# Attention and a feed-forward network in one kernel: the tiles that TensorE streams begin 64 bytes beyond its weights, modulo 256

## The chip, the cores and the metric

The kernel runs on one core of one Trainium2 chip. Its time is the device time of one launch in microseconds; three runs of the kernel before gave 839.77, 840.28 and 840.65 us, median 840.28 us.

## The reference

Four batch elements, 12 heads, 448 positions, head size 64; the model width is 768, and the feed-forward network is 3072 wide. All data are float32.

```
scores = q @ k^T / sqrt(64), causal mask, softmax over keys
x      = (softmax @ v), heads side by side          # (4, 448, 768)
xn     = (x - mean) / sqrt(var + 1e-6) * g_ln
out    = x + relu(xn @ w_ch1) @ w_ch2               # 768 -> 3072 -> 768
```

## The kernel before

**Products.** Every matrix is split into a high part and a low part of type float32r (`xh` and `xl`, `hh` and `hl`, `wh` and `wl`), and a product of two matrices is three matmuls into one PSUM bank: high by high, high weights by low data, low weights by high data. TensorE first loads a 128x128 weight tile (the stationary operand: LDWEIGHTS, PEld in the profile) and then streams the data past it (the moving operand, 448 or 450 columns of 4 bytes in each partition). Each matmul has a weight load of its own; the load of the next matmul runs while the present one streams.

**Stages.** Batches 0 and 1 run the plain network (function `ffn`): `ph` is the first product (data `xh`, `xl`), `po` the second (data `hh`, `hl`). In batch 0 `xh` and `xl` have 450 columns, two of them sums for the normalisation, and in batch 1 448. Batches 2 and 3 run together (class `Pair`) as seven products of sums and differences (Strassen's scheme); there the banks are `bX`, `bY`, `bA`, the weights `wk` and `wp`, and the data are `xh` and `xl` again (two of the seven), the tiles `xT1h`, `xT1l` to `xT4h`, `xT4l`, `xB22h` and `xB22l`, and for the second layer `h1` and `h2` (shown as `h`) and four tiles `hx`. The attention of a batch (`sc` scores, `pt` transposes, `px` the product with v) is spread among the network's matmuls of earlier batches.

**Order.** Nothing here is ordered by the hardware: the program is recorded whole (class `Plan`), list-scheduled by a table of costs on the five engines' queues, and written out in that order. All instructions carry the line of the recording helper (L553), so the profile is read by tiles. The change does not touch the costs or the dependences that the planner sees.

**Places in SBUF.** A tile pool gives each tile a fixed byte address in every partition, one after another. The two small tiles `least` and `ve`, and the big ones `xh` and `xl`, stand ahead of others in this row, so their sizes set the addresses of what follows. A product's chunk `c` begins 448 x 4 = 1792 bytes (7 x 256) after the one before it, so all chunks of a 448-column tile begin at the same byte modulo 256; with 450 columns each chunk begins 1800 bytes after the one before, 8 bytes further modulo 256. Weight chunks are 512 bytes long.

Of the kernel before, what the change touches and what calls it, by code (L numbers as in the profile page):

```python
# [11 lines left out]
F32 = mybir.dt.float32  # L12
F32R = mybir.dt.float32r
# [10 lines left out]
P = 128  # L24
C = 112
NC = S // C
NP = H // 2
KC = DM // P
# [533 lines left out]
def kernel(ctx, tc, qk, v, w1, w2, g, out):  # L562
# [3 lines left out]
    def pool(name, bufs, **kw):  # L566
        return Pool(plan, name, bufs, **kw)
# [6 lines left out]
    const = pool("const", 1)  # L574
    sb = pool("sb", 1)
# [18 lines left out]
    ident = identr.bitcast(F32)  # L594
    warm = const.tile([P, 1], BF16, name="warm")
    sums = const.tile([C, 5, 3, 4], F32, name="sums")
    least = const.tile([C, 6, 2], F32, name="least")
    mask = ap.tile([C, S], BF16, name="mask")
    g_sb = const.tile([P, KC + 1], F32, name="g_sb")
    g_sb, part = g_sb[:, :KC], g_sb[:, KC:]  # L600
# [79 lines left out]
    def move(dst, src):  # L680
        nc.either(
            ("scalar", "activation", (), dict(out=dst, in_=src, func=ACTF.Copy)),
            ("vector", "tensor_copy", (dst, src), {}),
        )
# [47 lines left out]
    class Att:  # L732
# [7 lines left out]

        def parts(self):
            n = S + 2 if self.b == 0 else S
            self.xh = sb.tile([P, KC, n], F32R, tag="xh", name="xh", bufs=1)
            self.xl = sb.tile([P, KC, n], F32R, tag="xl", name="xl", bufs=1)

        def columns(self):

# [257 lines left out]
        def squares(self):  # L1005
            if self.b in (1, 2):
                mb = self.spread_one(self.t["mv"])
                if self.b in MBS:
                    mb, wide = ap.tile([P, S], F32, tag="PT", name="mbs", bufs=8), mb
                    move(mb, wide)  # L1010
            else:
                mb = self.t["mb"] if self.b else self.mb
            some = [ap.tile([P, S], F32, tag="PT", name="xc", bufs=8) for _ in range(XC)]
            for c in range(KC):
                t = some[c % (XC - 1) + 1 if c else 0]
                nc.vector.tensor_tensor(out=t, in0=self.xT[c], in1=mb, op=ALU.subtract if self.b else ALU.add)
                nc.either(
                    ("scalar", "activation", (), dict(out=t, in_=t, func=ACTF.Square)),
                    ("gpsimd", "tensor_tensor", (), dict(out=t, in0=t, in1=t, op=ALU.mult)),
                )  # L1020
                if c:
                    self.add(acc, acc, t)
                else:
                    acc = t
            ve = sb.tile([C, NC], F32, tag="ve", name="ve", bufs=2)
            nc.vector.tensor_scalar_add(ve, self.small(acc, "var"), 1e-6)
            nc.gpsimd.tensor_tensor(out=ve, in0=ve, in1=mhalf, op=ALU.pow)
            self.t["ve"] = ve
# [575 lines left out]
```

## Time and profile before

| | kernel before |
|---|---|
| median of three runs | 840.28 us |
| span of the profiled execution, first to last instruction | 838.0 us |
| TensorE matmul busy | 830.5 us (99%), 4582 instructions |
| TensorE weight loads busy | 727.3 us |
| VectorE busy | 696.2 us (83%) |
| ScalarE busy | 513.0 us (61%) |
| GpSimd busy | 319.9 us (38%) |

The profiled execution's own time is its span; the launch around it is the 2.3 us by which the median stands above the span. TensorE's granted clock is at full in every slice of the page. A matmul's duration in the profile is its latency: the next one starts before it has ended, so what a matmul costs is the distance from its start to the start of the next one, and a run of matmuls is best read in the chain, where the pieces do not overlap.

### The profile page before, as it was taken

To read this page: it belongs to the slowest core of one execution; us is meant where nothing else is said; L and a number is where in the kernel's file an instruction comes from. 1 tells how busy PE (TensorE), PEld (TensorE's weight loads), DVE (VectorE), ACT (ScalarE), POOL (GpSimd) and SP (SyncE) were. 2 spreads that over 40 slices of the span, in tenths; PEclk is the share of its full clock that TensorE was granted. 3 is DMA by queue.
4 is the path that set the end of the run, shared out by engine and by line. 5 is a ranking of instruction groups with operands and counts; after the bars stand their busy time and mean duration, and the time that the engine had idled before them with its cause. 6 is when DMAs were issued, how large, how long until landed. Compare 5 with 4: busy or idle time off the path is not lost.

```text
span 838.0 us, 13712 instructions
## 1 busy us (share of the span) xinstructions
PE 830.5 (99%) x4582; PEld 727.3 (87%) x4582; DVE 696.2 (83%) x1445; ACT 513.0 (61%) x1129; POOL 319.9 (38%) x309
## 2 busy tenths in 40 slices
PE   9999999999999999999999999999999999999998
PEld 5679889888788898898989899999999898999997
DVE  6899999899999987877777489787887878778685
ACT  7999998888789675565454235543625435254450
POOL 5753111101452622421110378436446354554440
PEclk9999999999999999999999999999999999999999
DMA  9687888886778798769775464334243342423324
GB/s 200 257 298 257 316 281 313 319 298 252 268 268 299 236 332 274 275 221 293 241 232 191 149 200 136 117 101 123 74 138 95 103 121 85 147 74 116 117 92 149
DMA packets 61319, 168.79 MB, mean 201 GB/s; under 512 B 7009, under 2 KB 25825, under 8 KB 61249
## 3 DMA queue, kind: packets, MB, share of 16 engines
q1 hardware_dynamic: 61248, 167.92, 60.4%
q8 instruction: 36, 0.59, 0.3%
q14 instruction: 35, 0.28, 0.1%
HBM read 119.15 MB, written 39.71 MB: 190 GB/s over the span
## 4 chain that ended last, share of the span: by engine, by line
PE 95%; DVE 3%; ACT 1%; issue 0%; POOL 0%; ACTq 0%; POOLq 0%; DVEq 0%
PE po L553 21%; PE bX L553 21%; PE ph L553 21%; PE bY L553 11%; PE sc L553 5%; PE bA L553 5%; PE px L553 5%; PE pt L553 4%; DVE P L553 1%; DVE qs L553 1%; PE idle L553 0%; ACT rest L553 0%; PE rb L553 0%; PE var L553 0%; ACT PT L553 0%
## 5 line engine op out<-in xcount | busy, mean ns | idle before, releaser
L553 ACT ACTIVATE P<-P,least 112x112 f32<-112x112 f32 (+3 forms) x176 | 91.5, 524 | 35.9 <-DVE least L553 35.2
L553 PE MATMUL ph<-xh,wh 128*128 128x450 f32 (+1 forms) x288 | 109.0, 380 | 0.3 <-ACT wh L553 0.3
L553 PE MATMUL po<-hh,wh 128*128 128x448 f32 x288 | 108.5, 377 | 0.0
L553 PE MATMUL ph<-xh,wl 128*128 128x450 f32 (+1 forms) x288 | 106.9, 372 | 0.0
L553 PE MATMUL ph<-xl,wh 128*128 128x450 f32 (+1 forms) x288 | 106.4, 371 | 0.0
L553 PE MATMUL po<-hl,wh 128*128 128x448 f32 x288 | 105.8, 367 | 0.0
L553 PE MATMUL po<-hh,wl 128*128 128x448 f32 x288 | 105.6, 367 | 0.0
L553 POOL TENSOR_TENSOR kl<-qkraw,kh 128x896 fp32r<-128x896 f32 x18 | 40.6, 2255 | 158.9 <-ACT kh L553 105.5
L553 DVE CUSTOM_DVE_ANT_0 P<-sc,mask 112x112 f32<-112x112 f32 (+3 forms) x176 | 72.4, 441 | 24.7 <-PE sc L553 23.7
L553 ACT ACTIVATE wp<-s 128x256 fp32r<-128x256 f32 (+1 forms) x104 | 47.0, 462 | 69.9 <-PE bX L553 32.9
L553 POOL TENSOR_TENSOR s<-u 128x256 f32<-128x256 f32 (+1 forms) x60 | 56.1, 952 | 80.4 <-DMA u<-scratch 53.0
L553 ACT ACTIVATE wk<-u 128x256 fp32r<-128x256 f32 (+1 forms) x78 | 36.2, 465 | 74.0 <-PE bX L553 59.2
L553 DVE TENSOR_TENSOR wp<-s,wp 128x256 fp32r<-128x256 f32 (+1 forms) x120 | 71.3, 600 | 0.7 <-ACT wp L553 0.2
L553 POOL TENSOR_TENSOR h<-b,h 128x448 fp32r<-128x448 f32 x36 | 43.2, 1200 | 64.3 <-ACT h L553 34.8
L553 PEld LDWEIGHTS ph<-xh,wh 128*128 128x128 f32 x288 | 54.2, 188 | 6.0 <-ACT wh L553 0.6
L553 PEld LDWEIGHTS ph<-xh,wl 128*128 128x128 f32 x288 | 54.2, 188 | 5.1 <-issue 0.4
L553 PEld LDWEIGHTS po<-hh,wl 128*128 128x128 f32 x288 | 54.1, 188 | 4.6
L553 PEld LDWEIGHTS ph<-xl,wh 128*128 128x128 f32 x288 | 54.3, 189 | 4.1
L553 PEld LDWEIGHTS po<-hl,wh 128*128 128x128 f32 x288 | 54.3, 189 | 3.9
L553 PEld LDWEIGHTS po<-hh,wh 128*128 128x128 f32 x288 | 54.2, 188 | 3.9
L553 DVE TENSOR_TENSOR xT<-xT,bX 128x448 f32<-128x448 f32 x72 | 44.3, 616 | 13.2 <-PE bX L553 12.8
L553 ACT ACTIVATE PT<-pt 112x448 f32<-112x448 f32 x83 | 43.7, 541 | 17.0 <-PE pt L553 15.4
(190 smaller groups left out, 2220.3 us busy)
## 6 DMA issues: line engine op xcount, KB each, us to landing
raw<-w_dram SPq DMA_DIRECT2D x39, 768.0 KB, 6.3
scratch<-w SPq DMA_DIRECT2D x48, 384.0 KB, 3.6
full<-scratch SPq DMA_DIRECT2D x24, 768.0 KB, 7.1
qkraw<-qk_dram SPq DMA_DIRECT2D x18, 896.0 KB, 5.3
kept<-wl SPq DMA_DIRECT2D x30, 384.0 KB, 6.1
u<-scratch SPq DMA_DIRECT2D x24, 384.0 KB, 3.8
u<-scratch SPq DMA_DIRECT2D x36, 256.0 KB, 2.9
PR<-P SPq DMA_DIRECT2D x18, 490.0 KB, 6.6
```

The lines of the kernel that those rows point to most:

```text
L553: getattr(getattr(nc, t.engine), method)(*args, **kw)
```

## The change

Four tiles get other sizes, and through them the tiles behind them other addresses. No instruction is added, removed or moved: the programs have the same instructions in the same order on all engines.

```
-    least = const.tile([C, 6, 2], F32, name="least")
+    least = const.tile([C, 30, 2], F32, name="least")
...
             n = S + 2 if self.b == 0 else S
-            self.xh = sb.tile([P, KC, n], F32R, tag="xh", name="xh", bufs=1)
-            self.xl = sb.tile([P, KC, n], F32R, tag="xl", name="xl", bufs=1)
+            self.xh, self.xl = (
+                sb.tile([P, room], F32R, tag=x, name=x, bufs=1)[:, :KC * n].rearrange("p (c n) -> p c n", n=n)
+                for x, room in (("xh", 2752), ("xl", 2736))
+            )
...
-            ve = sb.tile([C, NC], F32, tag="ve", name="ve", bufs=2)
+            ve = sb.tile([C, 12], F32, tag="ve", name="ve", bufs=2)[:, :NC]
```

The addresses that the two programs give (byte in the partition, and the same modulo 256):

| tiles | read by TensorE as | before | after |
|---|---|---|---|
| `wh`, `wl`, `wk`, `wp`, eight buffers | weights | 113824 ... (160) | 114336 ... (160) |
| `hh`, `h1` | data | 17440 (32) | 17632 (224) |
| `hl`, `h2` | data | 38944 (32) | 39136 (224) |
| `xh` | data | 90400 (32) | 90592 (224) |
| `xl` | data | 101216 (96) | 101600 (224) |
| `hx`, four | data | 142016 ... (192) | 142560 ... (224) |
| `xT1h` to `xT4l`, `xB22h`, `xB22l` | data | 175584 ... (224) | the same (224) |
| `qs`; `kh`, `kl` | weights; data of the scores | 211168 (224); 214752, 218336 (224) | the same |

A block `i` of 112 queries in `qs` begins 448 x `i` bytes into it: block 0 at 224 modulo 256, block 2 at 96. The moving `kh` and `kl` always begin at 224.

So data begin 128 bytes (`hh`, `hl`, `h`, `xh`), 192 bytes (`xl`) or 32 bytes (`hx`) beyond the weights before, and 64 bytes afterwards. The tiles `xT1h` and so on stand at 64 bytes in both. The 450-column chunks of batch 0 stand at 128 to 168 (`xh`) and 192 to 232 (`xl`) before, and at 64, 72, ... 104 after, in both. Tiles that only the other engines and the DMAs use move by 192 to 576 bytes; their sizes, queues and instructions stay.

## Rows read from the trace of the kernel before

**Rows 1.** The page: busy time by engine, with its share and instructions.
```profile
PE 830.5 (99%) x4582; PEld 727.3 (87%) x4582; DVE 696.2 (83%) x1445; ACT 513.0 (61%) x1129; POOL 319.9 (38%) x309
```

**Rows 2.** What PE waited for: us in total, times, longest us.
```profile
PE sc L553 <- DVE qs L553: 1.7, 1, 1.7
PE idle L553 <- POOL warm L553: 0.9, 1, 0.9
```

**Rows 3.** The page's chain, by engine.
```profile
PE 95%; DVE 3%; ACT 1%; issue 0%; POOL 0%; ACTq 0%; POOLq 0%; DVEq 0%
```

**Rows 4.** PE's groups by form: count, busy us, mean latency ns, idle before.
```profile
L553 PE MATMUL po<-hh,wh 128*128 128x448 f32 x288 | 108.5, 377 | 0.0
L553 PE MATMUL ph<-xh,wh 128*128 128x450 f32 x144 | 54.9, 383 | 0.3 <-ACT wh L553 0.3
L553 PE MATMUL ph<-xl,wh 128*128 128x448 f32 x144 | 53.2, 369 | 0.0
L553 PE MATMUL bX<-h,wk 128*128 128x448 f32 x216 | 48.9, 366 | 0.0
L553 PE MATMUL bX<-hx,wp 128*128 128x448 f32 x108 | 27.8, 366 | 0.0
L553 PE MATMUL bA<-xh,wk 128*128 128x448 f32 x72 | 22.4, 365 | 0.0
```

**Rows 5.** The chain, batches 0 and 1: start us, us, what and how many.
```profile
89.97 7.40 PE ph L553 x36
114.86 7.34 PE po L553 x36
299.20 4.29 PE ph L553 x21
490.62 35.51 PE po L553 x174
```

**Rows 6.** The chain in the pair's stage, columns as in rows 5.
```profile
540.63 1.84 PE bA L553 x9
542.47 1.80 PE bX L553 x9
544.27 1.80 PE bY L553 x9
567.55 2.45 PE bX L553 x12
```

**Rows 7.** Timeline of PE there: start us, us, instruction with its tiles.
```profile
540.67 0.37 PE L553 MATMUL bA<-xl,wk 128*128 128x448 f32 x1
542.31 0.36 PE L553 MATMUL bX<-xT2h,wp 128*128 128x448 f32 x1
544.11 0.36 PE L553 MATMUL bY<-xT1h,wp 128*128 128x448 f32 x1
567.39 2.62 PE L553 MATMUL bX<-h,wk 128*128 128x448 f32 x12
574.12 0.77 PE L553 MATMUL bX<-hx,wp 128*128 128x448 f32 x3
574.72 1.38 PE L553 MATMUL bA<-h,wk 128*128 128x448 f32 x6
```

**Rows 8.** Timeline of PE, scores of a later batch within batch 1's first product.
```profile
307.93 0.21 PE L553 MATMUL sc<-kh,qs 128*112 128x112 f32 x1
307.98 0.26 PE L553 MATMUL sc<-kl,qs 128*112 128x112 f32 x1
308.08 0.36 PE L553 MATMUL sc<-kh,qs 128*112 128x336 f32 x1
308.28 0.41 PE L553 MATMUL sc<-kl,qs 128*112 128x224 f32 x2
```

**Rows 9.** Stretches: length, then busy us of PE, PEld, DVE, ACT, POOL; clock; DMA.
```profile
60.00:150.00 90.00, 90.00 (x511) 79.58 (x510) 85.77 (x175) 84.81 (x167) 16.90 (x9) 1.00 0.83 298
150.00:240.00 90.00, 88.30 (x516) 77.35 (x515) 82.31 (x174) 76.86 (x156) 23.27 (x16) 1.00 0.77 281
```

## The prediction

> **What bounds the kernel now.** I read the page's engine totals first, then PE's waits, the chain, and last the steps from one matmul to the next. PE is busy in 99% of a span of 838.0 us, DVE in 83% [rows 1]. Its waits for other engines are short: the longest is one wait of 1.7 us, the next 0.9 us at the start [rows 2], and the chain is PE in 95% [rows 3]. So the time is the sum of PE's steps, and the step (start of one matmul to start of the next) is what the change can touch. Latencies of some 370 ns [rows 4] are no price, since the next matmul starts long before.
>
> The reader is to see that these steps are not all alike, though all are 448 float32r columns at the full clock [rows 9]. In the pair's stage three pieces stand side by side: nine matmuls on `xh` and `xl` take 1.84 us, nine on `xT2` 1.80 us and nine on `xT1` 1.80 us [rows 6, 7]: 204.4 ns a step against 200.0 ns. Twelve on `h` take 2.45 us, 204.2 ns [rows 6, 7]. The weights are of the same tiles, the number of columns is the same; what differs is where the data begin. `xT1` and `xT2` begin 64 bytes beyond the weights modulo 256, `h` and `xh` 128, `xl` 192 (the table of addresses). After the change all products' data stand where `xT1` and `xT2` stand already. The trace of before thus holds its own trial of the change.
>
> **Is it the address modulo 256?** The fast tiles also lie elsewhere, above byte 175,000, while the others lie below the weights or just behind them; the pair's rows alone can't part the two reasons. The scores can. Their weights `qs` and data `kh`, `kl` all lie in the same high part. Two score matmuls of 112 columns follow each other: the one whose successor's weights begin at the data's own place modulo 256 (offset 0) takes 0.05 us to the next start, the one whose successor's weights stand 128 bytes off takes 0.10 us; the 336 columns behind it, again at 128, take 0.20 us, where 336/448 of 200.0 ns would be 150 ns [rows 8]. So the offset between the data that stream and the weights that load beside them costs time with no change of place. The price of an offset of 128 is 50 ns there and only some 4 ns in the network, so I take sizes from the network's own rows alone.
>
> Here a rule of the Trainium skill speaks against the change. "TensorE: Matmul & The Clock Gate", section "Step-by-step: what each phase is for", says that TensorE has one read port for the streamed data and another for weights, so that loading the next weights takes no read bandwidth from the running matmul. By that rule every offset gives one step, and the change moves nothing. The 0.05 against 0.10 us of rows 8 differ from it.
>
> **The change part by part.** No instruction is added, moved or taken away, so no engine gets a new wait or a new order; only steps change. The steps of `xT1` to `xT4` and `xB22` keep their addresses and cost nothing. The others:
> - `po`: 3 groups of 288 [rows 4], 864 steps. Now 7.34/36 = 203.9 and 35.51/174 = 204.1 ns [rows 5], call it 204.0; then 200.0. 864 x 4.0 ns = 3.5 us.
> - `ph` of batch 1: 3 groups of 144 at 448 columns [rows 4], 432 steps. Now 4.29/21 = 204.3 ns [rows 5]: 432 x 4.3 = 1.9 us.
> - `h` in the pair: 216 under `bX` with `wk` [rows 4], as many under `bY`, and 108 each under `bX` with `wp` and `bA`, 648 steps. 648 x 4.2 = 2.7 us.
> - `xh`, `xl` in the pair: 72 [rows 4], as many under `bX`, and half of that for `xl` in each, 216 steps. 216 x 4.4 = 1.0 us.
> - `hx`: 108 [rows 4]. Three take 0.60 us to the next start (574.12 to 574.72) [rows 7], 200 ns already; I count nothing.
> - `ph` of batch 0: 3 groups of 144 at 450 columns [rows 4], 432 steps of 7.40/36 = 205.6 ns [rows 5]. Only the first of six chunks lands at 64; at the rate of the fast tiles it would take 200.0 x 450/448 = 200.9 ns, so 72 x 4.7 = 0.3 us. The other 360 land at 72 to 104, where no network row stands. Bounds: the whole 4.7 ns (1.7 us), or nothing; lower still is the slower rival below. I take half, 0.85 us, since these offsets lie between a fast row (64) and a slow one (128), and keep 0 to 1.7. Together 1.15 us.
>
> The sum is 3.5 + 1.9 + 2.7 + 1.0 + 1.15 = 10.25 us. These rates are of undisturbed runs. A product at the edge of a run, next to a transpose or a score matmul, has its weights loaded late or beside other data, and gains nothing certain; the chain of batches 0 and 1 is broken into pieces of some 18 to 36 products [rows 5]. I take off a tenth, which leaves 9.2 us.
>
> **What stands beside it.** PE's gain counts in full where the others keep up. Between 60 and 240 us DVE is busy for 85.77 of 90 and 82.31 of 90 us [rows 9], and PE's longest wait was for DVE. About 2.6 us of the gain is batch 0's (432 of the `po` steps, 1.7 us, and the 1.15 us above, less a tenth), most of it there. DVE has 4.2 + 7.7 = 11.9 us idle in these 180 us, so it can follow on the whole, but at places it will be late: I take off 0.3 us. Later it is busy for less. The scores, transposes and `px` hold most of their addresses; where `PR` moves by 64 its chunks go through the same four places modulo 256 as before, and I count nothing. DMAs and the other engines read the same bytes in the same shapes, at other places; no row prices that, and I bound it by the differences between equal groups, well below 1 us either way, and take nothing.
>
> So 838.0 - 8.9 = 829.1 us of span. The median of the runs shown lies 2.3 us above the profiled span, which gives 831.4 us, 1.1% faster.
>
> **Rivals.**
> 1. No effect: the fast steps are fast for their place in SBUF or for the pair's pattern, and not for the offset. For it: all fast network rows lie in one part of the memory, and `hx`, at an offset of 32, can be as fast. Against it: rows 8, where the offset alone changes. Time: 840.3 us. The rule of the Trainium skill quoted above ("TensorE: Matmul & The Clock Gate") would give the same time.
> 2. DVE takes over in batch 0 and at the turn to batch 1: what PE gains there comes back as waits like the 1.7 us one [rows 2]. For it: DVE's 95% in one stretch [rows 9]; against it, its 11.9 us of idle time. Then 2.6 us of batch 0 are lost, and as much again if its lag reaches into batch 1: 834 to 836 us, still faster.
> 3. Slower: the 450-column chunks at 72 to 104 land on a bad offset. Both `xh` and `xl` move there, 360 steps. The scores show what a bad offset can cost: 50 ns a step [rows 8]. Without these chunks' gain the time is 831.4 + 0.8 = 832.2; with 360 x 50 ns = 18 us on top it is 850 us. It decides from 8.1/360 = 23 ns a step. For it: these places are unseen. Against it: today's chunks also step by 8 bytes, through 128 to 168 and 192 to 232, and their mean of 205.6 ns shows no such place among them.
>
> **How the numbers follow.** The forecast gets 0.74, rival 1 0.10, rival 2 0.11, rival 3 0.05. The likeliest's own range is 829 to 834 us: with no discount and all of the 450-column gain it is 838.0 + 2.3 - 11.1 = 829.2, with the latter at nothing and twice the discounts 833.5. The range reaches to 828.5 (steps a little faster than 200.0 ns) and to 837.5, which takes in rival 2, and leaves out rivals 1 and 3. A measurement tells about 0.2%, 1.7 us, from no change. The forecast and rival 2 are faster; a very small part of them would fall within 0.2%. That makes 0.84 faster, 0.11 the same, 0.05 slower.
>
> **What would show it.** Right: `po`, `h` and `ph` of batch 1 at some 200 ns a step (36 in 7.2 us, twelve in 2.40), `xT1` and `xT2` unchanged at 1.80 for nine; PE's waits still a few us; DVE's idle share smaller. For rival 1 the steps stay at 204; for rival 2 they fall and PE's waits grow by as much; for rival 3 pieces of `ph` with 36 steps take 7.5 us or more in batch 0. I am wrong if the steps depend on the absolute place of data and weights, or on the order of tiles, so that equal offsets give unequal steps.

## The result, and the profile after

| | before | after |
|---|---|---|
| median | 840.28 us (839.77 to 840.65, 4 runs) | 833.05 us (832.71 to 833.43, 4 runs) |
| ratio to before, 95% interval | | 0.9912 (0.9898 to 0.9926) |
| span of the profiled execution | 838.0 us | 830.7 us |

The change takes 7.2 us off the time, 0.9%; 8.9 us were forecast. On another chip the changed kernel gave 0.9912 (0.9898 to 0.9927) again, 832.72 us.

The page's engine totals of the changed kernel, against [rows 1]:

```profile
span 830.7 us, 13712 instructions
PE 823.4 (99%) x4582; PEld 727.2 (88%) x4582; DVE 694.5 (84%) x1445; ACT 512.2 (62%) x1129; POOL 319.4 (38%) x309
```

PE lost 7.1 us of busy time, DVE 1.7 and ACT 0.8; the instruction counts are the same. What PE waited for, against [rows 2] (us in total, times, longest us):

```profile
PE sc L553 <- DVE qs L553: 1.7, 1, 1.7
PE idle L553 <- POOL warm L553: 0.9, 1, 0.9
```

No wait of PE has grown. VectorE (DVE, the third engine in the row) in the stretch from 60 to 150 us, against [rows 9], where it had 85.77 us:

```profile
60.00:150.00 90.00, 90.00 (x513) 80.02 (x512) 86.34 (x176) 85.04 (x169) 17.38 (x9) 1.00 0.83 298
```

The chain of the changed kernel (start us, us, what and how many), against [rows 5, 6]:

```profile
90.16 7.39 PE ph L553 x36
114.95 7.21 PE po L553 x36
298.18 4.21 PE ph L553 x21
487.51 34.83 PE po L553 x174
...
536.74 1.80 PE bA L553 x9
538.54 1.80 PE bX L553 x9
540.34 1.80 PE bY L553 x9
...
555.02 2.40 PE bX L553 x12
```

Here the reader sees the whole result: `po` went from 7.34 to 7.21 us for 36, from 35.51 to 34.83 for 174 (200.2 ns a step), the nine `bA` on `xh` and `xl` from 1.84 to 1.80, twelve `bX` on `h` from 2.45 to 2.40. The nine on `xT2` and `xT1`, whose addresses stayed, keep 1.80. Only the 450-column `ph` of batch 0 hardly moved: 7.40 to 7.39.

Both programs have the same matmuls in the same order, so each step (start to the next start) of one trace can be taken from the same step of the other. Summed by what streams ("within runs" means that the next matmul writes the same bank, with the few steps of over 220 ns left out; the sums take all steps):

| steps | mean step within runs, before and after | difference of the sums, us | forecast, less a tenth |
|---|---|---|---|
| `po` (864) | `hh` 204.2, `hl` 203.2; 200.1, 201.0 | -2.37 | -3.1 |
| `ph`, 448 columns (432) | `xh` 204.4, `xl` 205.2; 200.7, 200.5 | -1.47 | -1.7 |
| `h` in the pair (648) | 203.5; 200.2 | -1.94 | -2.4 |
| `xh`, `xl` in the pair (216) | 203.5; 200.0 | -0.76 | -0.9 |
| `hx` (108) | 203.4; 200.0 | -0.37 | 0 |
| `ph`, 450 columns (432) | 205.8; 204.8 | -0.29 | -1.0 |
| all steps of PE | | -7.24 | -9.2 |

What remains in the last row cancels out: the scores take 0.30 us more, and `xB22h`, whose address stayed, 0.34 us less, most of it at three steps that took about 300 ns in the trace of before; the rest is near nothing. So PE's steps make up all of the 7.3 us of span.

### The profile page after: what moved, and what is told of

It reads as the page before. It is cut to its first block, busy times and chain, and to the rows that moved or that the text cites. A ratio compares the mean times of both kernels' runs of the same rounds, so it can differ in the third digit from the quotient of the medians.

```text
span 830.7 us, 13712 instructions
## 1 busy us (share of the span) xinstructions
PE 823.4 (99%) x4582; PEld 727.2 (88%) x4582; DVE 694.5 (84%) x1445; ACT 512.2 (62%) x1129; POOL 319.4 (38%) x309
## 4 chain that ended last, share of the span: by engine, by line
PE 95%; ACT 2%; DVE 2%; issue 0%; POOL 0%; ACTq 0%; POOLq 0%; DVEq 0%
PE po L553 21%; PE bX L553 21%; PE ph L553 21%; PE bY L553 11%; PE sc L553 5%; PE bA L553 5%; PE px L553 5%; PE pt L553 4%; DVE P L553 1%; ACT PT L553 1%; PE idle L553 0%; ACT P L553 0%; DVE qs L553 0%; ACT rest L553 0%; PE rb L553 0%; PE var L553 0%
## 5 line engine op out<-in xcount | busy, mean ns | idle before, releaser
L553 DVE TENSOR_TENSOR wp<-s,wp 128x256 fp32r<-128x256 f32 (+1 forms) x120 | 67.9, 572 | 0.9 <-ACT wp L553 0.2
```

The lines of the kernel that those rows point to most:

```text
L553: getattr(getattr(nc, t.engine), method)(*args, **kw)
```

## The experiments

**The offset by itself.** A kernel with nothing but runs of 36 matmuls, each with its own weight load, and the data begun at a chosen distance from the weights modulo 256; it computes nothing of the network. (This code and the pieces below are shortened.)

```
+for off in range(0, 256, 16):                       # a<off>b
+    for i in range(36):
+        nc.tensor.matmul(psum[i % 2], lhsT=near[:, 128 * (i % 8):][:, :128],
+                         rhs=near[:, 1152 + off // 4:][:, :448], start=True, stop=True)
```

> A measurement by itself, nothing of the network is computed: runs of 36 float32r matmuls of 448 columns, each with its own weight load, in which the data begin 0, 8, 16, ... 240 bytes beyond the weights modulo 256; then 450 columns, 112 columns, data far away in the memory, weights themselves at 64, 128 or 192, and last with VectorE and ScalarE working beside. Theory A (the offset between the data and the next weights, modulo 256, sets the step): about 200 ns at 64 and 204 to 206 at 128 and 192, a smooth or stepped curve between; the same by offset when data lie far away or when the weights are moved; at 450 columns a rise from 64 to 104. Theory B (the data's own place modulo 256): with the weights at 64, 128, 192 the fast offset moves. Theory C (the distance in the memory): near data equal at every offset, far data faster. Theory D (the offset counts only where other engines use the memory as well): all offsets equal until VectorE and ScalarE run beside.

The chain of that kernel. The names say the offset: `a` 448 columns, `n` 112, `f` data some 130 KB away from the weights, `v64x128` weights at 64 and data 128 beyond them:

```profile
15.56 7.55 PE a0b L47 x36
45.44 7.34 PE a64b L47 x36
75.28 7.46 PE a128b L47 x36
90.28 7.33 PE a160b L47 x36
247.40 3.71 PE n0b L47 x36
254.81 3.71 PE n128b L47 x36
269.88 7.33 PE f64b L47 x36
277.22 7.47 PE f128b L47 x36
292.09 7.34 PE v64x64b L47 x36
299.43 7.47 PE v64x128b L47 x36
```

TensorE's granted clock is 1.00 from 15 to 336 us. Each run holds some 0.14 us more at its ends (at 64 its first step takes 312 ns, its last 220); within runs the mean step is 200.1 ns at 64, 200.0 at 160, 203.9 at 128, 202.0 at 192, 206.7 at 0. The offset counts (theory A). It counts with the data near or far alike, so not the distance (C falls), and with no other engine at work (D falls). Over all the offsets tried at 448 columns the mean runs from 200.0 ns to 208.3 (at 72), with no smooth curve between.

The timeline of PE in the last part, where VectorE and ScalarE run beside (start us, us, what):

```profile
344.83 7.48 PE L47 MATMUL b64b<-near 128*128 128x448 f32 x36
352.16 7.61 PE L47 MATMUL b128b<-near 128*128 128x448 f32 x36
359.62 7.55 PE L47 MATMUL b192b<-near 128*128 128x448 f32 x36
```

From start to start 64 takes 7.33 us and 128 takes 7.46 us, as without them. At 112 columns all four offsets take 3.71 us: no effect there, which matters below. At 450 columns, where every matmul of a run has the same offset, 64 and 72 take 200.0 ns each and 80 takes 206.7 ns:

```profile
187.56 7.32 PE w64b L47 x36
202.22 7.57 PE w80b L47 x36
```

**Weights moved in place of the data.** Against the kernel before:

```
-    self.xh = sb.tile([P, KC, n], ...); self.xl = sb.tile([P, KC, n], ...)
+    xh in a room of 2748 elements, xl in one of 2736     # weights to 224, xl to 32
-    ve = sb.tile([C, NC], F32, tag="ve", name="ve", bufs=2)
+    ve = sb.tile([C, 12], F32, tag="ve", name="ve", bufs=2)[:, :NC]
```

> The kernel before with the data left at 32 modulo 256 (xl brought to 32 too) and the weights moved from 160 to 224, so that the data stand 64 bytes beyond them as in the changed kernel; xT1 to xT4 and xB22 stand at offset 0. Theory A: po, h and 448-column ph fall to about 200 ns a step, and the time is that of the changed kernel, 833 us, give or take 2 us for xT1 to xT4 at offset 0. Theory B (the data's own place, 224, is the fast one): po, h and ph stay at 204 ns, xT1 to xT4 at 200, and the time stays at 840 us.

Measured: 835.66 us, 0.9946 (0.9929 to 0.9962). Its chain:

```profile
115.38 7.21 PE po L553 x36
487.97 34.83 PE po L553 x174
537.33 1.80 PE bA L553 x9
539.13 1.82 PE bX L553 x9
```

With data still at 32, `po` and `bA` run as in the changed kernel, to the last digit; `bX` on `xT2`, never touched but now at offset 0, lost its 1.80 (step by step `xT1` to `xT4` and `xB22` rose from 199 to 201 ns to 202 to 205 ns, and cost 2.2 us). So the place of the data against the weights counts and neither's own (B falls). The time is a little beyond the 835 us that A allowed; 2.2 of the 2.6 us more than in the changed kernel are the tiles that now stand wrong.

**Other offsets in the network.** The changed kernel with other sizes of the same tiles:

```
offset 0:    least [C, 22, 2]; xh, xl in rooms of 2748, 2752; ve [C, 4]
offset 160:  least [C, 10, 2]; xh, xl in rooms of 2748, 2712; ve [C, 40]
```

> The changed kernel with hh, hl, h, xh and xl at the weights' own place modulo 256 (offset 0), hx at 32. Theory A: the scores' steps at offset 0 had no excess, so 0 should be no slower than 64: po and h at 197 to 201 ns a step, 830 to 834 us. Theory B: the place 160 is not the fast one, so 204 ns and 838 to 841 us. If two accesses at the same place modulo 256 are what collides, offset 0 is the worst, above 206 ns a step, and the time is over 842 us.

Measured: 838.87 us, 0.9989 (0.9980 to 0.9998). Its chain:

```profile
115.09 7.42 PE po L553 x36
490.36 35.28 PE po L553 x174
```

The step is 206.1 ns in one stretch and 202.8 in another, 203.4 ns in the mean: the guess that offset 0 is free, drawn from the scores, was wrong. The rival under which it is the worst is wrong as well; it is about as good as 128.

> The changed kernel with the data of hh, hl, h, xh, xl and hx 160 bytes beyond the weights in place of 64 (xT1 to xT4 and xB22 stay at 64). Theory A: 160 was as good as 64 in the sweep, so po, h and ph with 448 columns take 200 to 201 ns a step and the time is that of the changed kernel, 833 us within 1. Rival (64 is good for another reason than its step in the sweep, or the sweep's steady runs do not carry over to a network with other engines): 203 to 205 ns and 838 to 841 us.

Measured: 837.24 us, 0.9962 (0.9948 to 0.9976); the changed kernel on the same chip took 832.72. Its chain:

```profile
115.51 7.21 PE po L553 x36
489.36 35.96 PE po L553 x174
539.90 1.86 PE bA L553 x9
```

This is the most telling of all. The same matmuls at the same offset take 200.3 ns in the first piece and 206.7 ns in the second. Of 160 the first sweep had seen the good level alone. So an offset can have two levels, and what chooses between them is not settled. It is also the sign that the prediction named for itself last: equal offsets with unequal steps.

**The network's own pattern.** A second kernel with matmuls alone: runs near 64 and 160, the pattern of three products over six chunks at 448 (`t`) and 450 columns (`w`, chunks 8 bytes apart), and the scores' sequence of widths.

```
+for c in range(6):
+    for w, x in ((WH, XH), (WH, XL), (WL, XH)):
+        mm(t, w + 128 * c, x + off // 4 + c * cols, cols)      # t<off>b, w<off>b
+for i in (3, 0, 2, 1, 1, 3, 0, 2):
+    for x in (XH, XL):
+        mm(t, places[i], x, 112 * (i + 1), wc=112)             # own: 112 * i; one: 0
```

> A measurement by itself, nothing of the network is computed. First runs of 36 equal-offset matmuls of 448 columns at 52 to 76 and 152 to 168 bytes, then the network's own pattern (six chunks, each high weights by high data, high by low, low by high) at 448 columns and, for each start from 0 to 248 bytes in steps of 8, at 450 columns, where chunks stand 8 bytes apart; last the scores' sequence of widths, once with weights at their own places and once all at one place. Theory A, as the first sweep left it (64 and 160 are the good offsets, by the place of data against weights alone): 200.0 ns at 60 to 68 and at 160, over 202 a few bytes away; the pattern of three at 448 columns 200 ns at 64 and 160, 203 to 207 at 0 and 128; at 450 columns no start under 203 ns, since six chunks never stand all at a good offset. Rival (the step depends on what came before it, not on the offset of the pair): the pattern of three differs from the plain runs at equal offsets, and some start at 450 columns may reach 201 ns. For the scores: if the offset made their long steps, the sequence with all weights at one place (offset 0) has none of them; if the order of widths made them, both sequences show the same steps.

Its chain:

```profile
47.72 7.21 PE a64b L35 x36
54.94 7.44 PE a68b L35 x36
62.38 7.21 PE a76b L35 x36
84.30 7.44 PE a160b L35 x36
...
106.69 7.29 PE t0b L35 x36
113.98 7.21 PE t64b L35 x36
121.19 7.34 PE t128b L35 x36
128.54 7.20 PE t160b L35 x36
...
165.12 7.31 PE w32b L35 x36
194.46 7.36 PE w64b L35 x36
```

Offset 160 stands at 7.44 here and at 7.20 in the pattern of three: two levels again, though the plain runs of the two sweeps are not quite alike (here all matmuls of a run write one PSUM bank and there are six weight tiles, there two banks in turn and eight). 64 stands at 200 ns wherever it was tried with 448 columns and 128 weight columns. Four bytes further (68) the run is on the upper level, and at 76 on the lower: the curve is no smooth one. At 450 columns with the chunks 8 bytes apart the best of the 32 starts, 32, takes 203.0 ns, much as theory A had it, and 64, that of the changed kernel, 204.4.

The two sequences of the scores take the same time (2.26 and 2.24 us for 16), and step by step nearly the same lengths (one step of 336 columns differs by 9 ns), though one has its weights at four places and the other at one:

```
own: ... 51   96  209  150  104  105 ...
one: ... 50   98  200  152  103  103 ...     (ns; widths 112 112 336 336 224 224)
```

So the 0.05 and 0.10 us of [rows 8] come from the order of widths, not from the offset.

**Part of the change undone.** The changed kernel with `xh` and `xl` put back to 128 and 192 beyond the weights:

```
-    sb.tile([P, room], ...)[:, :KC * n]       for ("xh", 2752), ("xl", 2736)
+    sb.tile([P, room], ...)[:, 16:16 + KC * n] for ("xh", 2768), ("xl", 2720)
```

> The changed kernel with xh and xl alone put back to where they stood against the weights (128 and 192 bytes beyond them, their 450-column chunks 8 bytes further each); hh, hl, h and hx stay at 64. Theory A (each product's step is set by its own offset, and PE's steps add up to the time): the matmuls on xh and xl go back to 203 to 206 ns, which the two traces price at 0.84 + 0.59 us in batch 1's first product, 0.76 us in the pair and 0.33 us in batch 0's, so 2.5 us more than the changed kernel, 835.4 us; po and h stay at 200 ns. Rival (other engines give back what PE gains, so that the parts do not add up): less than 1 us or more than 4 us of difference.

Measured: 836.14 us, 0.9952 (0.9938 to 0.9965). Its chain:

```profile
115.46 7.21 PE po L553 x36
298.92 4.30 PE ph L553 x21
489.68 34.83 PE po L553 x174
539.01 1.86 PE bA L553 x9
```

`po` stays as changed, `ph` and `bA` are as before. Step by step these matmuls cost 2.6 us more than in the changed kernel; the time differs by 3.1 to 3.4 us. The rest of the traces' difference (0.35 us at the first scores, 0.25 us at three steps of `xB22h`) lies in tiles that this edit does not move, and such steps differ from trace to trace: one of `xB22h` took 282 ns before, 201 in the changed kernel and 275 here. The parts add up, within these sizes.

**Does the load of the weights hold the data up?**

```
+for cols in (256, 320, 384, 512, 448): run(f"c{cols}x{off}b", off, cols=cols)    # off 64, 128, 0
+for wc in (32, 64, 96, 128): run(f"l{wc}x{off}b", off, wc=wc)                    # 448 columns
```

> A measurement by itself, nothing of the network is computed: runs of 36 float32r matmuls at offsets 64, 128 and 0, with 256 to 512 columns of data at 128 weight columns, then with 32 to 128 weight columns at 448 columns of data. Theory A1 (the data are held up only while the next weights load beside them): the excess of a step over the columns at full clock (columns/2.4 ns) is the same at every number of columns, about 13 ns at offset 64 and 17 ns at 128, and shrinks with fewer weight columns. Theory A2 (the data are held up all along, by a slower reading of their own): the excess grows with the columns of data, from 8 ns at 256 to 15 ns at 512, and does not depend on the weight columns.

Its chain:

```profile
15.66 4.29 PE c256x64b L44 x36
19.95 4.49 PE c256x128b L44 x36
28.96 5.49 PE c320x64b L44 x36
34.45 5.46 PE c320x128b L44 x36
...
112.24 7.47 PE l32x64b L44 x36
119.71 7.34 PE l32x128b L44 x36
```

Neither theory holds. The excess at offset 64 is 6.7 ns at 256 columns (113.3 a step against 106.7), 13.3 at 320, 13.2 at 384, 13.3 at 448, 15.6 at 512: not constant (A1), not in proportion (A2). With 32 weight columns instead of 128 the excess does not shrink, and 64 becomes the worse offset (206.7 against 202.6 ns). At 320 columns the offset is without effect, and at 512 offset 0 is the best of the three (227.7 ns against 229.0 at 64). With 64 weight columns offset 64 leads by 1.0 to 1.5 ns, with 96 it does not lead. So 64 is good for 448 columns with weights of 128, not as such.

The same kernel holds the plainest case of two levels. It runs 448 columns with 128 weight columns at 64, 128 and 0 twice, once in each series; the matmuls are the same. The timeline of PE:

```profile
104.54 7.70 PE L44 MATMUL c448x0b<-near 128*128 128x448 f32 x36
193.27 7.58 PE L44 MATMUL l128x0b<-near 128*128 128x448 f32 x36
```

Within runs offset 0 takes 206.7 ns the first time and 202.8 the second, while 64 and 128 repeat within 0.3 ns. So neither the offset nor the 72 matmuls just before decide between the levels.

## Why the prediction was right, and where its sizes were off

- **PE's steps set the time:** right. Their differences sum to 7.24 us, the span fell by 7.3, the median by 7.2.
- **448-column data at 64 run at 200.0 ns:** right, 200.2 in the network. The trace of before did hold its own trial.
- **The step from before, 204.0 to 204.4 ns:** the main size that was off. I took long pieces of the chain. Over all steps within runs the means are 203.2 and 204.2 for `po` and 203.5 for `h`, so `po` and `h` gained 0.7 and 0.5 us less than the sum less a tenth. That one offset can stand on two levels, as the run at 160 shows, may be why a few pieces mislead.
- **The tenth for edges:** right in kind and too small for `po` and `ph`. 169 of the 864 steps of `po` and 99 of the 432 of batch 1's `ph`, a fifth, have a score, a transpose or `px` just before or behind them; their sums changed by 0.01 and 0.05 us, so nearly all of the gain is in the rest.
- **450 columns, 1.15 us:** the term that was mis-sized most; it measured 0.29. Not even the first chunk, at 64, came near 200.9 ns (204.4 on average): in the pattern of batch 0 the chunks' offsets change every third matmul, and a good one among others is not enough, as the second sweep shows (204.4 ns at the same start), though 450 columns can run at 200.0 ns where every matmul has offset 64 (first sweep). Rival 3, a bad offset at 23 ns or more, did not come up: the worst chunk, at 104, takes 207.2 ns.
- **`hx`, nothing:** off by 0.37 us; one row of 0.60 us was read, and the mean before was 203.4 ns.
- **VectorE, 0.3 us:** not needed; PE's waits are the same, though VectorE went up to 86.34 of 90 us between 60 and 150 us, so rival 2 is out. This deduction and `hx` made up for 0.7 us of what the other terms had too much.
- **Rows 8 as proof of the offset:** wrong. The step named there, that only the offset differs between 0.05 and 0.10 us, failed: the order of widths makes these steps. What it was to prove, that the offset counts and not the place in the memory, is shown by the sweeps and by the weights moved. Rival 1 deserved more than 0.10 on what rows 8 could tell. And the offset is not the whole of it: at 0 and at 160 equal offsets gave unequal steps, the prediction's own sign of being wrong. It came out right because 64, the offset that the fast tiles of before already had, held its level in every run with 448 columns and 128 weight columns.

The rule of the Trainium skill ("TensorE: Matmul & The Clock Gate", section "Step-by-step: what each phase is for"), that the load takes no read bandwidth from the running matmul, would give no effect of the offset; the runs show one of 3 to 4 ns in 200. What goes on beneath is open: the last sweep does not support a plain collision with the load.

No version tried is faster than the changed kernel. One with the 450-column chunks 2048 bytes apart, all at offset 64, was not tried; it needs some 3 KB more in each partition. An estimate from the first sweep's 200.0 ns and the 205.1 ns of the 324 steps of `ph` in batch 0 that have products on both sides: some 1.7 us.

## What to carry to other kernels

Where PE never waits, compare the steps of equal matmuls from start to start, by the tile that streams: a few ns times thousands is the whole gain to be had. Where SBUF tiles begin against each other can be such a few ns; a kernel that has some groups at another place carries the trial in its own trace. Take the mean over all steps of a group, not the longest pieces, count the steps at the edges of runs, which may gain nothing, and try the good place for the very width and weight columns in use, more than once, since it need not be good for others and a place can have two levels.

## What the runs showed of the hardware that was not expected

Many of the steady runs stand on the same few levels: 200.0 or 206.7 ns at 448 columns, 113.3 or 120.0 at 256, 146.7 at 320. These are multiples of 6.67 ns, which is 16 columns, or 64 bytes of float32, if a column takes one cycle of 2.4 GHz (an estimate); 448 columns would then be 28 of them (186.7 ns), and these runs take 30 or 31. Not all runs stand there: at offset 56 the steps are all 204 or 205 ns and at 156 all 203 or 204, and at 128 they vary from 196 to 212 with a mean of 203.9. The same offset can stand on either of two levels (160: 200.3 and 206.7 ns in one execution; 0: 206.7 and 202.8 ns for the same matmuls); of the offsets tried more than once with 448 columns and 128 weight columns only 64 always had the lowest. And steady runs of 112-column matmuls with 112 weight columns step at 98.3 ns at all four offsets tried, about twice the 46.7 ns that 112 columns would take by the same estimate.
